# A fused transformer block in fp32: the negative row maxima of the attention are turned behind the second group of value products, in two column groups, and no longer between two score pairs

## The chip, the cores and the metric

The kernel runs on one core of one Trainium2 chip. The metric is the time of one execution in device microseconds (us), as the median of several executions. All arithmetic is in fp32, with fp32r (a rounded fp32) for the large products, which are split into a high and a low part.

## The reference

What is computed is one block with adaptive layer norm: attention with 32 heads of 16 over 2048 rows of 512, then a gated feed-forward part of width 1792.

```python
mod = (_silu(c) @ w_mod).reshape(c.shape[0], 6, 1, -1)
sa, ca, ga, sb, cb, gb = (mod[:, 0], mod[:, 1], ...)
h = _layernorm(x) * (1 + ca) + sa
x = x + ga * attention(h, A_wqkv, A_wo)      # softmax over 2048 keys, 32 heads of 16
h = _layernorm(x) * (1 + cb) + sb
x = x + gb * ((_silu(h @ B_w_gate) * (h @ B_w_up)) @ B_w_down)
```

The softmax is the ordinary one: the maximum of each score row is taken off before the exponential.

## The kernel before, in words

**Tiling.** The attention runs over 32 units. A unit is a group of four heads against 512 queries; it has 16 steps, one for each 128 keys. A step makes four score products (one for each head, L568: keys on the output's partitions, 512 queries along its columns), four exponentials of them on ScalarE (L570) and the value products (L583) that multiply the exponentials with the values. Values and a column of ones are 17 columns of each head, so that a value product has 32 output partitions: the four heads of a group stand beside each other in four column groups of TensorE, each with all 128 rows. A score product has a contraction of 50 rows only and uses half of TensorE's rows.

**The maxima.** The row maxima have to be known ahead of the exponentials. So the kernel computes the scores a second time, 21 steps ahead (`LEAD`), with queries on the partitions: a product on the other half of the rows (L521, 48 rows) into a PSUM bank, and a reduction of that bank on VectorE (L523). There are four banks for these products (numbers 0 to 3, `four`), and three (numbers 4 to 6, `bank`) for the scores whose exponentials ScalarE takes. A *pair* is one score product and one product for a maximum (`pair_of`); the two stand in different halves of TensorE's rows and run side by side.

**Windows.** `plain` runs steps in which there is no other product to fill TensorE with. It goes by windows: three pairs (`WIN`), then one or two half steps of value products (`pvs`; a half step is four matmuls), then what is due at the end of a step (`end_steps`). Over four windows the half steps are 2, 2, 1, 1, so four windows are three steps, and the four windows are called W1 (followed by eight value products), W2 (followed by eight), W3 (followed by four) and W4 (followed by four) below. `filled` runs steps between whose pairs products of the output projection and the feed-forward part are taken.

**Turning the maxima.** When the last maximum of a unit is known, every query has its maxima in one column of `m` (128 partitions by 16). The scores take them off inside the product: two more rows of the contraction (rows 48 and 49 of `qop`) hold minus the maximum as a rounded part `nm` and the rest, and the key operand has ones there. So 16 columns of 128 have to become rows. Where a step has filler, VectorE does that (`max_turned`). Where it has none, `max_rows` does: VectorE takes the maximum over four blocks (L528), ScalarE makes the rounded negative (L540), and three TensorE matmuls with 16 stationary columns (L533 to L535) write the rounded part and the rest into two column ranges of one bank of the three for the scores; ScalarE copies the bank (L537) and SyncE's queue sends two small DMAs into `qop` (L539). The work is put into the list `side`, of which one entry is taken after each pair: the three matmuls come behind the fifth entry's pair, thus two pairs into the second window after the maximum, with the third pair behind them.

**Order.** The instructions of each engine stand in the order in which this code issues them; nothing moves them later. An engine runs its queue in that order, and waits where an operand or a bank isn't ready.

Of the kernel before, what the change touches and what calls it, by code (L numbers as in the profile page):

```python
# [9 lines left out]
F32 = mybir.dt.float32  # L10
F32R = mybir.dt.float32r
# [8 lines left out]
P = 128  # L20
# [18 lines left out]
KR = 48  # L39
# [20 lines left out]
def take(it, k):  # L60
    run(islice(it, k))
# [40 lines left out]
def block_kernel(ctx, tc, x, wqkv, wo, w_gate, w_up, w_down, c, w_mod, out):  # L102
    nc = tc.nc
# [18 lines left out]
    four, bank, single = Turn(0, 1, 2, 3), Turn(4, 5, 6), Turn(7)  # L122

    ident = const.tile([P, P], F32, name="ident")
    minus = const.tile([P, P], F32, name="minus")
# [228 lines left out]
    bank = Turn(4, 5, 6, 7)  # L354
# [101 lines left out]
    for ci in range(NC - 1):  # L456
# [6 lines left out]
        if ci == 1:  # L463
            bank = Turn(4, 5, 6)
# [25 lines left out]
    pb = ctx.enter_context(tc.tile_pool(name="pb", bufs=2, reuse_waits="tile"))  # L490
    kop[1] = pb.tile([P, 2, S], F32R, name="kop1", bufs=1)
    pf = None
    qop, mx, pts, pv, o_, due, res = {}, {}, {}, {}, {}, {}, {}
    posts = []
    n = 16 * NU
    last = NC - 1

# [27 lines left out]
    def max_rows(u):  # L525

        m = pb.tile([P, 16], F32, name="m", tag="m")
        nc.vector.tensor_reduce(m, mx.pop(u).rearrange("p b s t f -> p (b s t) f"), op=ALU.max, axis=AX.X)  # L528
        nm = pb.tile([P, 16], F32R, name="nm", tag="nm")

        def rows():
            pr = bank("pr")[0:16, 0:2 * P]
            nc.tensor.matmul(pr[:, 0:P], nm.bitcast(F32), ident, start=True, stop=True)  # L533
            nc.tensor.matmul(pr[:, P:2 * P], m, minus, start=True, stop=False)  # L534
            nc.tensor.matmul(pr[:, P:2 * P], nm.bitcast(F32), minus, start=False, stop=True)  # L535
            mr = pb.tile([16, 2, P], F32R, name="mr", tag="mr", bufs=1)
            nc.scalar.copy(mr, pr.rearrange("p (r q) -> p r q", r=2))  # L537
            for r in range(2):
                nc.sync.dma_start(qop[u][KR + r:KR + r + 65:64].bitcast(F32), mr[:, r, :].bitcast(F32))  # L539
        side.extend([lambda: None, lambda: None, lambda: nc.scalar.mul(nm, m, -1.0), lambda: None, rows])  # L540

    def max_turned(u, scale=nc.scalar.mul):

# [28 lines left out]
    def pv_step(i, half):  # L572

        u, kt = divmod(i, 16)
        g = u % NG
        cols = slice(half * HQ, (half + 1) * HQ)
        if kt == 0 and half == 0:
            pv[u] = single("pv")
            o_[u] = pf.tile([P, CW], F32, name="o", tag="o", bufs=2)
        p_ = pts.pop(i) if half else pts[i]  # L580
        for h in range(4):
            e0 = (kt * H + 4 * g + h) * (DH + 1)
            nc.tensor.matmul(pv[u][32 * h:32 * h + 32, cols], v_flat[:, e0:e0 + 32], p_[h][:, cols],  # L583
                             start=(kt == 0 and half == 0), stop=(kt == 15),
                             skip_group_check=half == 1)
        if kt == 15 and half:
            nc.scalar.copy(o_[u], pv[u])
# [285 lines left out]
    side = []  # L873
# [20 lines left out]
    def hook():  # L894
        while posts:
            posts.pop(0)()
# [7 lines left out]
    four, bank = Turn(0, 1, 2, 3, 6, 7), Turn(4, 5)  # L904
# [4 lines left out]
    def close_unit(u, i):  # L909

        if u == NU - 1:
            res[u] = out_a(u, nc.scalar)
            return
        res[u] = out_a(u, nc.sync)
        if u + 3 < NU:
            load_k(u + 3)
            load_q(u + 3)
        i0 = i if u % NG == NG - 1 else i + 3
        at(i0 + 3, lambda: res.__setitem__(u, out_b(u, nc.sync, *res[u])))
        at(i0 + 4, lambda: res.__setitem__(u, out_r(u, nc.sync, *res[u])))  # L920
        at(i0 + 5, lambda: out_c(u, nc.gpsimd, nc.gpsimd, *res.pop(u)))
        if u % NG == NG - 1:
            if u // NG:
                at(i + 4, lambda: begin(u // NG))
                at(i + 5, lambda: chunks[u // NG].load_wo())
            at(i + 7, lambda: chunks[u // NG].load_o(nc.gpsimd))
            at(i + 9, lambda: chunks[u // NG].split_o())
# [7 lines left out]
    def after(i):  # L935
        nonlocal pf
        for f in due.pop(i, []):
            f()
        j = i + LEAD
        if j % 16 == 15 and j < n:  # L940
            if i < -1:
                max_turned(j // 16, nc.vector.tensor_scalar_mul)
            else:
                (max_turned if beside else max_rows)(j // 16)
        if i == -2:
            run(late)
            sm.finish()
            es_a0.close()
            pf = ctx.enter_context(tc.tile_pool(name="pf", bufs=1, side="right", reuse_waits="tile"))
            kop[2] = pf.tile([P, 2, S], F32R, name="kop2")  # L950
            ones_rows(2)
            load_k(2)
            load_q(2)
        if 0 <= i < UG and i % 16 in ((3, 5, 8) if i < UG - 16 else (1, 3, 5)):
            next(weights2, None)
# [5 lines left out]
    def pair_of():  # L961
        nonlocal done
        i = done // 4 - 1
        most = 4 * n - 4 * (LEAD - 1)
        h = (ORDER if done < most else (0, 1, 2, 3))[done % 4]
        work = [lambda: score(i + 1, h)]
        if done < most:
            work.insert(1 - h % 2, lambda: max_one(done + 4 * (LEAD - 1)))
        for f in work:
            f()  # L970
        done += 1
        if side:
            side.pop(0)()

    for i in range(-LEAD, -1):
# [7 lines left out]
        if i == -2:  # L983
            four, work = three, bank
            for k in range(4):
                bank = Turn(7, 3, 6)
                for _ in range(WIN):
                    pair_of()
                bank = work
# [6 lines left out]
    def pvs(most, by_halves):  # L996

        nonlocal owed
        if by_halves:
            most, owed = most + owed, 0  # L1000
        while most and halves and 4 * halves[0][0] + 8 <= done:
            i, half = halves.pop(0)
            pv_step(i, half)
            most -= 1
            if i % 16 == 15 and half:
                close_unit(i // 16, done // 4 - 1)
                if by_halves:
                    break
        if by_halves and most and halves and 4 * halves[0][0] + 8 <= done:
            owed = most  # L1010

    def end_steps():
        nonlocal ended
        while ended < done // 4:
            after(ended - 1)
            ended += 1

    def plain(steps, tails=()):

        nonlocal four, bank, beside  # L1020
        beside = False
        assert steps % WIN == 0 and done % 4 == 0
        four, bank = Turn(0, 1, 2, 3), Turn(4, 5, 6)
        for w in range(4 * steps // WIN):
            for _ in range(WIN):
                pair_of()
            if w >= 4 * steps // WIN - len(tails):
                tails[w - 4 * steps // WIN](four())
            pvs((HALVES[(w - 2) % 4] if done > 8 else 0) + (w == 4 * steps // WIN - 1), True)
            end_steps()  # L1030

    def filled(places, work):

        nonlocal four, bank, beside
        beside = True
        four, bank = three, Turn(4, 5)
        if done >= 4 * n - 4 * (LEAD - 1):
            places, bank = ALONE.get(places, places), Turn(4, 5, 0, 1, 2)
        for r in range(len(places)):
            pair_of()  # L1040
            take(work, places[r])
            if r % 4 == 3:
                end_steps()
        hook()
        pvs(6, False)

    def two_of(u):
        return [kop[u % 3][:, e, :].rearrange("p (k c) -> p k c", k=NK) for e in range(2)]
# [11 lines left out]
    for ci in range(last):  # L1060
        plain(STARTS[ci] - done // 4)
        ch = chunks[ci]
        for t0 in (0, 2):
            work = out_pair(ch, t0, outs, True)
            filled(TWO, work)
            filled(TWO, work)
        side.append(lambda: scaled(ch))
        plain(NORM)
        plain(WIN, [lambda tp, k=k: ch.turned(tp, k) for k in range(NK)])
        if ci == last - 1:  # L1070
            plain(REST)
        for _ in range(len(ch.jobs) - (KEEP if ci == last - 1 else 0)):
            job, args = ch.jobs.pop(0)
            if args == (NF // FG - 1, 0):
                plain(WIN)
            work = job(ch, *args, outs, True)
            for places in (TWO, TWO) if job is gate_up else (DOWN,):
                filled(places, work)
# [80 lines left out]
```

## Time and profile before

| what | value |
|---|---|
| median of 3 runs | 1838.07 us (1837.73 to 1839.37) |
| the profiled execution | 1838.88 us, its span on the core 1837.1 us |
| granted TensorE clock | 1.0 of full speed in the profiled span |
| turns by `max_rows` (L533 to L535) | 16 of 32 units, between 203.4 and 1457.5 us |
| mean of one reduction for a maximum (L523) | 681 ns, 2048 of them |

How to read it: the span is the time from the first to the last instruction on the core; what lies around it is start and end of the execution. In the profile an engine's busy time is the union of its instructions. A fp32 matmul of the turn or of the values stands as two records (two passes), a score product as one. The timeline merges consecutive instructions of one form: "x42" is a run of 42, its time runs from the first one's start to the last one's end, and a bracket shows the idle time ahead of it and what ended it. Names such as PE, PEld, DVE, ACT, POOL and SP are TensorE's matmuls, its weight loads, VectorE, ScalarE, GpSimd and SyncE.

### The profile page before, as it was taken

The page shows a single profiled execution, that of the slowest core. Times are in us where ns is not written, and L with a number is a line of the kernel's source. Part 1 is how long each engine was busy: PE and PEld are TensorE (multiplying, and loading weights), DVE is VectorE, ACT ScalarE, POOL GpSimd, SP SyncE. Part 2 cuts the span into 40 slices and gives each one's busy share as a digit, 9 for nine tenths or more (in the row PEclk, how much of TensorE's full clock was granted, in tenths as well). Part 3 has the DMA queues.
Part 4 walks back from the last instruction along what each step waited for, and adds up shares of the span by engine and source line. Part 5 has one row for each costly group of instructions (what it writes and reads, how often), then busy time and mean ns, then how long its engine had stood idle before and what let it go on. Part 6 is the DMA issues. An engine that isn't in the chain of part 4 may idle for free.

```text
span 1837.1 us, 41048 instructions
## 1 busy us (share of the span) xinstructions
PE 1825.5 (99%) x16904; PEld 1198.2 (65%) x16904; DVE 1532.5 (83%) x2578; ACT 1243.7 (68%) x2386; POOL 460.4 (25%) x541
## 2 busy tenths in 40 slices
PE   9999999999999999999999999999999999999999
PEld 7876444444455777776565777776564577777887
DVE  5578999999999888889999888889999988831544
ACT  4223888888877777777878777777878877774211
POOL 3612544565223111111123111111123011130200
PEclk9999999999999999999999999999999999999999
DMA  8884876657845444453544554444643545333642
GB/s 305 286 225 149 183 185 199 168 189 178 209 79 125 102 120 141 118 147 70 149 103 105 134 132 116 123 117 90 158 81 57 111 93 149 138 122 121 271 169 110
DMA packets 80488, 267.63 MB, mean 146 GB/s; under 512 B 19604, under 2 KB 24212, under 8 KB 59620
## 3 DMA queue, kind: packets, MB, share of 16 engines
q1 hardware_dynamic: 61324, 179.71, 33.8%
q0 software_dynamic: 18288, 84.49, 19.3%
q8 instruction: 133, 2.18, 0.5%
q10 hardware_dynamic: 688, 0.80, 0.2%
q14 instruction: 55, 0.45, 0.1%
HBM read 201.85 MB, written 62.13 MB: 144 GB/s over the span
## 4 chain that ended last, share of the span: by engine, by line
PE 96%; DVE 2%; ACT 1%; DMA 1%; SPq 0%; issue 0%; DVEq 0%
PE bank L583 27%; PE bank L781 19%; PE bank L568 18%; PE bank L521 14%; PE bank L791 8%; PE bank L211 7%; DVE mx L523 1%; PE bank L824 1%; DMA wm_ab<-in_w_mod 1%; PE bank L765 0%; DVE stt L807 0%; PE bank L533 0%; PE bank L163 0%; PE bank L534 0%; PE bank L535 0%
## 5 line engine op out<-in xcount | busy, mean ns | idle before, releaser
L523 DVE TENSOR_REDUCE mx<-bank 128x1 f32<-128x512 f32 x2048 | 1276.0, 681 | 108.5 <-PE bank L521 66.2
L568 PE MATMUL bank<-qop,kop 50*128 50x512 f32 x2048 | 730.2, 425 | 1.0 <-ACT pt__16517 L570 0.2
L521 PE MATMUL bank<-kop,qop 48*128 48x512 f32 x2048 | 726.6, 425 | 2.9 <-DVE mx L523 2.6
L568 PEld LDWEIGHTS bank<-qop,kop 50*128 50x128 f32 x2048 | 342.6, 184 | 169.9 <-issue 55.6
L521 PEld LDWEIGHTS bank<-kop,qop 48*128 48x128 f32 x2048 | 343.5, 184 | 113.9 <-DVE mx L523 67.7
L781 PE MATMUL bank<-act,wgu 64*128 64x512 f32 x1872 | 300.9, 392 | 0.0
L781 PEld LDWEIGHTS bank<-act,wgu 64*128 64x128 f32 x1872 | 196.1, 187 | 24.7 <-issue 0.2
L610 POOL TENSOR_TENSOR on<-o,rb 128x512 f32<-128x512 f32 x31 | 39.8, 1284 | 498.1 <-DMA rb<-d_dr 363.6
L781 PE MATMUL bank<-wd,mid 64*128 64x512 f32 x912 | 134.0, 397 | 0.0
L843 POOL CAST mid<-m 128x512 fp32r<-128x512 f32 x40 | 24.3, 608 | 379.3 <-DVE m L841 176.5
L781 PEld LDWEIGHTS bank<-wd,mid 64*128 64x128 f32 x912 | 88.0, 185 | 15.9 <-ACT first L878 3.2
L211 PE MATMUL bank<-hT,wqs 128*128 128x512 f32 x384 | 94.3, 397 | 0.4 <-DVE wqs L351 0.4
L839 DVE SCALAR_TENSOR_TENSOR q<-th,bank 128x512 f32<-128x512 f32 x56 | 38.2, 682 | 54.4 <-ACT th L835 54.4
L211 PEld LDWEIGHTS bank<-hT,wqs 128*128 128x128 f32 x384 | 70.7, 188 | 18.8 <-issue 2.9
L835 ACT ACTIVATE th<-bank 128x512 f32<-128x512 f32 x56 | 33.3, 594 | 58.1 <-PE bank L791 58.1
L855 DVE TENSOR_TENSOR x<-bank,x 128x512 f32<-128x512 f32 x84 | 53.9, 685 | 18.3 <-PE bank L781 16.8
L841 DVE TENSOR_TENSOR m<-bank,q 128x512 f32<-128x512 f32 x56 | 38.7, 691 | 21.7 <-PE bank L791 19.7
L844 POOL TENSOR_TENSOR mid<-m,mid 128x512 fp32r<-128x512 f32 x40 | 51.5, 1287 | 3.3
L791 PE MATMUL bank<-wd,mid 128*128 128x512 f32 x216 | 51.4, 393 | 0.0
L211 PE MATMUL bank<-wqs,hT 128*128 128x512 f32 x192 | 48.0, 398 | 0.0
L781 PE MATMUL bank<-wgu,act 64*128 64x512 f32 x288 | 47.8, 394 | 0.1
L791 PEld LDWEIGHTS bank<-wd,mid 128*128 128x128 f32 x216 | 40.3, 188 | 9.1 <-POOL mid L844 0.3
(6298 smaller groups left out, 5133.0 us busy)
## 6 DMA issues: line engine op xcount, KB each, us to landing
wgu<-gu_dr SPq DMA_DIRECT2D x48, 1024.0 KB
wd<-wd_dr SPq DMA_DIRECT2D x28, 1024.0 KB
kop<-kd SPq DMA_DIRECT2D x33, 768.0 KB
kop<-kd POOLq DMA_DIRECT2D x29, 768.0 KB, 8.8
gu_dr<-wgu POOLq DMA_DIRECT2D x14, 1024.0 KB, 13.5
kd<-prt SPq DMA_DIRECT2D x16, 512.0 KB
qd<-prt SPq DMA_DIRECT2D x16, 512.0 KB
kop<-gu_dr SPq DMA_DIRECT2D x8, 1024.0 KB
```

The lines of the kernel that those rows point to most:

```text
L211: nc.tensor.matmul(pt, lhs(a, k), rhs(b, k), start=(n == 0), stop=(n == 3 * nk - 1))
L521: nc.tensor.matmul(pm, qop[u][rows, s, qt * P:(qt + 1) * P], kop[u % 3][rows, s, kc * CW:(kc + 1) * CW], start=True, stop=True)
L523: nc.vector.tensor_reduce(mx[u][:, b, s, qt, kc:kc + 1], pm, op=ALU.max, axis=AX.X)
L568: nc.tensor.matmul(sp, kop[u % 3][rows, h // 2, kt * P:(kt + 1) * P], qop[u][rows, h // 2, :], start=True, stop=True)
L583: nc.tensor.matmul(pv[u][32 * h:32 * h + 32, cols], v_flat[:, e0:e0 + 32], p_[h][:, cols], start=(kt == 0 and half == 0), stop=(kt == 15), ...
L610: mul.tensor_mul(on, o, rb)
L781: nc.tensor.matmul(outs[e], lhs(e, a, k)[rows], rhs(b, k)[rows], start=(ph == 0 and j == 0), stop=(j == z and (ph == 1 or trade is not None)),
L791: nc.tensor.matmul(outs[e], lhs(e, a, k), rhs(b, k), start=(j == 0), stop=(j == z))
L839: nc.vector.scalar_tensor_tensor(q, th, 1.0, outs[0], op0=ALU.add, op1=ALU.mult)
L841: nc.vector.tensor_mul(m32, outs[1], q)
L844: (nc.gpsimd if slow else nc.vector).tensor_sub(mid[:, 1, :], m32, mid[:, 0, :].bitcast(F32))
L855: nc.vector.tensor_add(ch.x2[:, t, :], outs[e], ch.x2[:, t, :])
```

## The change

`rows`, the part of `max_rows` with the three matmuls, is no longer an entry of `side`. It is put into a new list `behind` with a count of 2; `plain` and `filled` call `turns_behind` behind each group of value products, which counts down and runs it at 0. So the matmuls now stand behind the second group of value products after the maximum. The two results go to two column groups instead of two column ranges: the rest to output partitions 32 to 47, the rounded part to 0 to 15, and the order of the three matmuls is rest, rounded, rest. The copy on ScalarE is 48 partitions by 128 columns instead of 16 by 256. Lines behind L540 have numbers one higher in the changed kernel (L568 is L569, L583 is L584).

```diff
-    posts = []
+    posts, behind = [], []
...
         def rows():
-            pr = bank("pr")[0:16, 0:2 * P]
-            nc.tensor.matmul(pr[:, 0:P], nm.bitcast(F32), ident, start=True, stop=True)
-            nc.tensor.matmul(pr[:, P:2 * P], m, minus, start=True, stop=False)
-            nc.tensor.matmul(pr[:, P:2 * P], nm.bitcast(F32), minus, start=False, stop=True)
-            mr = pb.tile([16, 2, P], F32R, name="mr", tag="mr", bufs=1)
-            nc.scalar.copy(mr, pr.rearrange("p (r q) -> p r q", r=2))
+            pr = bank("pr")[:, 0:P]
+            nc.tensor.matmul(pr[32:48], m, minus, start=True, stop=False)
+            nc.tensor.matmul(pr[0:16], nm.bitcast(F32), ident, start=True, stop=True)
+            nc.tensor.matmul(pr[32:48], nm.bitcast(F32), minus, start=False, stop=True)
+            mr = pb.tile([48, P], F32R, name="mr", tag="mr", bufs=1)
+            nc.scalar.copy(mr, pr[0:48])
             for r in range(2):
-                nc.sync.dma_start(qop[u][KR + r:KR + r + 65:64].bitcast(F32), mr[:, r, :].bitcast(F32))
-        side.extend([lambda: None, lambda: None, lambda: nc.scalar.mul(nm, m, -1.0), lambda: None, rows])
+                nc.sync.dma_start(qop[u][KR + r:KR + r + 65:64].bitcast(F32), mr[32 * r:32 * r + 16].bitcast(F32))
+        side.extend([lambda: None, lambda: None, lambda: nc.scalar.mul(nm, m, -1.0)])
+        behind.append([2, rows])
...
+    def turns_behind():
+        for b in list(behind):
+            b[0] -= 1
+            if not b[0]:
+                b[1]()
+                behind.remove(b)
...
             pvs((HALVES[(w - 2) % 4] if done > 8 else 0) + (w == 4 * steps // WIN - 1), True)
+            turns_behind()
             end_steps()
...
         hook()
         pvs(6, False)
+        turns_behind()
```

The order on TensorE at the first turn (before: 203.4 us of the span). Here the second window is W1, eight value products follow it, and `bank_67` to `bank_69` are the three banks of the scores. Before:

```order
L521 MATMUL bank_66<-kop_1509,qop 128x512
L568 MATMUL bank_67<-qop,kop_88 128x512
L568 MATMUL bank_68<-qop,kop_88 128x512
L521 MATMUL bank_63<-kop_1509,qop 128x512
L533 MATMUL bank_69<-ident,nm 16x128
L534 MATMUL bank_69<-minus,m 16x128
L535 MATMUL bank_69<-minus,nm 16x128
L568 MATMUL bank_67<-qop,kop_88 128x512
L521 MATMUL bank_64<-kop_1509,qop 128x512
L583 MATMUL bank_70<-pt__1774,v_flat 32x256
```

The three matmuls stand between the second and the third pair of the window here. The same place with the change, from the end of W1's eight value products to the third pair of W2:

```order
L584 MATMUL bank_70<-pt__1787,v_flat 32x256
L584 MATMUL bank_70<-pt__1799,v_flat 32x256
L533 MATMUL bank_67<-minus,m 16x128
L534 MATMUL bank_67<-ident,nm 16x128
L535 MATMUL bank_67<-minus,nm 16x128
L521 MATMUL bank_65<-kop_1509,qop 128x512
L569 MATMUL bank_68<-qop,kop_88 128x512
L521 MATMUL bank_66<-kop_1509,qop 128x512
L569 MATMUL bank_69<-qop,kop_88 128x512
L569 MATMUL bank_67<-qop,kop_88 128x512
```

The three matmuls have moved by one pair and eight value products; the third score of the next window now takes the bank that the turn has used.

The third turn (before: 282.1 us), where the second window is W4 with four value products behind it. With the change:

```order
L521 MATMUL bank_64<-kop_971,qop 128x512
L521 MATMUL bank_65<-kop_971,qop 128x512
L569 MATMUL bank_68<-qop,kop_1509 128x512
L584 MATMUL bank_70<-pt__2772,v_flat 32x256
L584 MATMUL bank_70<-pt__2792,v_flat 32x256
L584 MATMUL bank_70<-pt__2777,v_flat 32x256
L584 MATMUL bank_70<-pt__2797,v_flat 32x256
L533 MATMUL bank_69<-minus,m 16x128
L534 MATMUL bank_69<-ident,nm 16x128
L535 MATMUL bank_69<-minus,nm 16x128
L521 MATMUL bank_66<-kop_971,qop 128x512
```

Before, the three stood ahead of the pair with `bank_65`; now that pair and the four value products are ahead of them, and W1 follows.

On ScalarE one exponential moves ahead of the copy, here at the first turn with the change:

```order
L571 ACTIVATE pt__1832<-bank_67 128x512
L571 ACTIVATE pt__1835<-bank_68 128x512
L571 ACTIVATE pt__1840<-bank_69 128x512
L537 CAST mr<-bank_67 48x128
L571 ACTIVATE pt__1862<-bank_68 128x512
```

Before, the copy came ahead of the third exponential. The orders of VectorE, GpSimd and SyncE's queue are the same as before.

## The prediction

> **What bounds the kernel now.** I read the head of the page first, then the busy time by stretches, with the stretch of windows without filler from 195 to 530 us beside one with filler (605 to 860 us), and then the timelines of VectorE and TensorE around the turns.
>
> ```profile
> span 1837.1 us, 41048 instructions
> PE 1825.5 (99%) x16904; PEld 1198.2 (65%) x16904; DVE 1532.5 (83%) x2578; ACT 1243.7 (68%) x2386; POOL 460.4 (25%) x541
> ...
> core 0: us, PE busy (x) PEld busy (x) DVE busy (x) ACT busy (x) POOL busy (x), PEclk, DMA share, GB/s
> 195.00:530.00 335.00, 334.84 (x3364) 161.70 (x3368) 332.86 (x568) 292.37 (x577) 168.73 (x172) 1.00 0.68 180
> 605.00:860.00 255.00, 255.00 (x2710) 187.77 (x2701) 225.82 (x370) 181.14 (x347) 38.01 (x45) 1.00 0.50 124
> ...
> L533 PE MATMUL bank<-ident,nm x32: 272/278/283, 203.4 to 1457.5; 128*16 128x128 f32 x32
> ```
>
> The 99% of PE says little: with filler it is 100% too, and VectorE (DVE) has 29 us of 255 to spare there. Without filler VectorE is idle for 2.1 us of 335. So in the stretches where the turns stand it is VectorE's chain of reductions that sets the time, and TensorE only costs what it makes VectorE wait. The 32 records of L533 are 16 turns of two passes; by their starts all 16 lie in such stretches, between 203 and 1457 us. [...]
>
> What VectorE waits, turn by turn:
>
> ```profile
> L523 DVE TENSOR_REDUCE mx<-bank 128x1 f32<-128x512 f32 x2048 | 1276.0, 681 | 108.5 <-PE bank L521 66.2 <-PE bank L568 34.1
> ...
> 202.26 3.67 DVE L523 TENSOR_REDUCE mx<-bank 128x1 f32<-128x512 f32 x6
> ...
> 206.14 25.35 DVE L523 TENSOR_REDUCE mx<-bank 128x1 f32<-128x512 f32 x42 [0.21 <-PE bank L568]
> 246.31 25.32 DVE L523 TENSOR_REDUCE mx<-bank 128x1 f32<-128x512 f32 x42 [0.24 <-PE bank L521]
> ...
> 280.75 26.15 DVE L523 TENSOR_REDUCE mx<-bank 128x1 f32<-128x512 f32 x43
> ...
> 565.74 9.41 DVE L523 TENSOR_REDUCE mx<-bank 128x1 f32<-128x512 f32 x15
> ```
>
> Six reductions in a row take 3.67 us and the last one 0.68, so one follows the other after (3.67 - 0.68) / 5 = 0.598 us, 0.08 us before its forerunner's record ends. A bracket of 0.21 us therefore is a loss of 0.29, and a run of n that lasts longer than 0.598 (n - 1) + 0.68 has lost the rest inside. By where the turn falls in the four windows there are four kinds:
>
> - **A**, turn in W1 (203.4, 320.4, 437.3, 1457.4 us; 4 of 16): 0.29 + (25.35 - 25.20) = 0.44 us.
> - **B**, in W3 (244.0, 360.9, 477.9; 3): 0.24 + 0.08 + (25.32 - 25.20) = 0.44.
> - **C**, in W4 (282.1, 399.1, 516.0, 921.9, 1327.9, 1419.2; 6): 26.15 - (42 x 0.598 + 0.68) = 0.35.
> - **D**, in W3 of the short stretches that begin with a layer norm (566.6, 972.5, 1378.5; 3): 9.41 - (14 x 0.598 + 0.68) = 0.36.
>
> Together 1.76 + 1.32 + 2.10 + 1.08 = 6.26 us. That is all there is to win on VectorE.
>
> **The change part by part.** What a turn costs TensorE, in a place of kind C:
>
> ```profile
> 281.69 0.39 PE L568 MATMUL bank<-qop,kop 50*128 50x512 f32 x1
> 282.14 0.39 PE L533 MATMUL bank<-ident,nm 128*16 128x128 f32 x2
> 282.37 0.38 PE L534 MATMUL bank<-minus,m 128*16 128x128 f32 x2
> 282.59 0.38 PE L535 MATMUL bank<-minus,nm 128*16 128x128 f32 x2
> 282.90 0.50 PE L521 MATMUL bank<-kop,qop 48*128 48x512 f32 x1
> ...
> 212.99 0.61 PE L521 MATMUL bank<-kop,qop 48*128 48x512 f32 x2
> 213.22 0.40 PE L568 MATMUL bank<-qop,kop 50*128 50x512 f32 x1
> ```
>
> From pair to pair it is 282.90 - 281.69 = 1.21 us with a turn and 0.23 without one (212.99 to 213.22): about 0.95 us are **removed**. What is **added** behind value products:
>
> ```profile
> 212.10 0.38 PE L583 MATMUL bank<-pt__1870,v_flat 128*32 128x256 f32 x1
> 212.11 0.38 PE L583 MATMUL bank<-pt__1890,v_flat 128*32 128x256 f32 x1
> ...
> 212.32 0.38 PE L583 MATMUL bank<-pt__1870,v_flat 128*32 128x256 f32 x1
> ...
> 212.65 0.50 PE L521 MATMUL bank<-kop,qop 48*128 48x512 f32 x1
> ```
>
> Products of different column groups start 0.01 us apart, and the next four 0.22 us behind; then a pair comes after 0.33. A turn there starts 0.22 us behind the last four, its first two matmuls stand in different column groups and share 0.22 us (one matmul's step, 282.37 to 282.59), and the pair comes 0.31 us after the third (282.59 to 282.90). So 0.22 + 0.22 + 0.31 - 0.33 gives a delay of **0.42 us**. Its bounds: not under 0.42, since the first and the third matmul share a column group and its bank; 0.64 if the two don't overlap.
>
> What this delay does depends on how long a bank has lain ready before its reduction begins, its lead:
>
> ```profile
> 205.61 0.49 PE L521 MATMUL bank<-kop,qop 48*128 48x512 f32 x1
> ...
> 214.55 0.73 PE L521 MATMUL bank<-kop,qop 48*128 48x512 f32 x2
> ...
> 215.26 6.66 DVE L523 TENSOR_REDUCE mx<-bank 128x1 f32<-128x512 f32 x11
> ...
> 216.35 0.46 PE L568 MATMUL bank<-qop,kop 50*128 50x512 f32 x1
> 216.81 0.49 PE L568 MATMUL bank<-qop,kop 50*128 50x512 f32 x1
> 217.47 0.38 PE L583 MATMUL bank<-pt__1926,v_flat 128*32 128x256 f32 x1
> 217.80 0.50 PE L521 MATMUL bank<-kop,qop 48*128 48x512 f32 x1
> 218.28 0.18 PEld L568 LDWEIGHTS bank<-qop,kop 50*128 50x128 f32 x1 [0.18 <-ACT pt__2007 L570]
> ...
> L528 DVE TENSOR_REDUCE m<-mx x16: 204/206/220, 202.1 to 1456.1; 128x16 f32<-128x64 f32 x16
> ```
>
> The least lead is 206.14 - (205.61 + 0.49) = 0.04 us. In windows without a turn the first bank of W2 is ready at 212.65 + 0.50 = 213.15; it is the 13th of the run from 206.14, so its reduction begins at 206.14 + 12 x 0.598 + 0.15 = 213.47: lead 0.32. The first bank of W3 is ready at about 214.55 + 0.50 = 215.05 and reduced at 215.26: lead 0.21. That is the tightest place, 0.17 us above the least, since two groups of eight products lie before it. In W4 TensorE is ahead and waits for banks: the third pair comes 216.81 - 216.35 = 0.46 us behind the second instead of 0.23. In W1 its third score waits 0.18 us for an exponential, which costs about 0.08 of the window. So:
>
> - **A now** stands between W1's eight products and W2. Nothing absorbs the delay up to W3: loss 0.42 - 0.17 = 0.25 us (0.14 at W2, 0.11 at W3). Gain 0.44 - 0.25 = 0.19.
> - **C now** stands between W4 and W1. W4's wait is behind it; W1's wait for the exponential absorbs about 0.08. Loss 0.42 - 0.08 - 0.17 = 0.17; gain 0.18.
> - **B and D now** stand between W3 and W4. There W4's wait of 0.23 absorbs it, and so does the 0.21 us by which the maximum over four blocks (L528) has just put VectorE back and lengthened every lead: 0.44 for 0.42. Loss 0; gain 0.44 and 0.36.
>
> Sum: 4 x 0.19 + 6 x 0.18 + 3 x 0.44 + 3 x 0.36 = 0.76 + 1.08 + 1.32 + 1.08 = **4.2 us**.
>
> The rest is costed at nothing, with its cover:
>
> ```profile
> 217.56 0.67 ACT L570 ACTIVATE pt__2007<-bank 128x512 f32<-128x512 f32 x1
> ...
> 283.00 0.36 ACT L537 CAST mr<-bank 16x256 fp32r<-16x256 f32 x1
> ...
> L539 SPq DMA_DIRECT2D qop<-mr x32: 525/538/565, 204.7 to 1459.2; - x32
> ```
>
> *The copy* began 0.41 us behind the third matmul (282.59 to 283.00) and took 0.36 us; with half the columns it lies between this and 0.23 us (the 16 columns of `nm`), and I take 0.25. The third score of the next window now waits for it. Laid onto the rows at 217: turn at 217.69, third matmul 217.91, copy from 218.32 (the exponential before it ended at 218.23) to 218.57, or 218.68 at most; the third score is due at 217.91 + 0.31 + 0.57 = 218.79, and a score started 0.05 us after the exponential it waited for. That leaves 0.06 to 0.17 us of cover. Each 0.1 us beyond it costs about 0.1 per turn of kinds A and C. *The DMAs* are the same two in the same place of SyncE's queue. At most a pair and eight products later, some 1.3 us, they land for scores that come five steps later, 20 reductions or 12 us; each issue takes 0.54 us. *The negative* (L540) ends before and TensorE no longer waits for it.
>
> The profiled execution took 1838.88 us, 0.81 over the median of 1838.07: 1838.88 - 4.2 = 1834.7 there, and **1833.9 us** against the median.
>
> **The rivals.**
>
> 1. *TensorE is the bound after all.* Then each turn is worth 0.95 - 0.42 = 0.53 us, 8.5 in all: 1829.6. For it: PE at 99%. Against it: VectorE's 2.1 idle us in 335. Chance 0.04.
> 2. *Everything VectorE loses comes back*, if TensorE's waits absorb more than I count in A and C: 6.26 us, 1831.8. The waits for banks in W1 and W4 speak for it, the two groups of eight products behind them against it. Chance 0.13.
> 3. *The two column groups don't overlap*: delay 0.64. A loses 0.47, C 0.39, B and D about 0.03 (0.64 - 0.44 - 0.17): 1.88 + 2.34 + 0.18 = 4.4, gain 1.9, 1836.2. Against it: the value products' starts 0.01 us apart. [...] Chance 0.13.
> 4. *Slower: the third score waits for ScalarE's copy*, because exponentials stand before it. With one more (0.49 us, less the cover of 0.06) each turn delays TensorE by 0.43 us more: A loses 0.68, C 0.60, B and D, with 0.25 of it absorbed, about 0.2: 2.7 + 3.6 + 1.2 = 7.5 instead of 6.26, so 1839.3; with two more, about 8 us on top, 1847. It outweighs the gain from about 0.35 us of delay on. For it: ScalarE runs back to back in W4 (217.56 to 218.23). Against it: that exponential ends before the copy could begin. Chance 0.08.
> 5. *It is hidden*: what VectorE gains is waited for where stretches with filler begin: 1838. Against it: they begin with TensorE at work, not with a DMA. Chance 0.07. That the turns don't move at all is excluded by the order, where 16 of 16 have moved.
>
> **How the numbers follow.** The forecast has 0.55. Its own range is 1832.8 to 1835.2: leads may be off by 0.1 us in the ten turns of A and C, and the cover may be short. About 0.2%, 3.7 us, is what a measurement of this kernel tells from no change, that is 1834.4; two thirds of the forecast's chance (0.37) lie below it. Faster is 0.37 + 0.04 + 0.13 = 0.54, the same 0.18 + 0.13 + 0.07 = 0.38, slower 0.08. The range for 8 in 10 goes from the second rival, 1831.6, to just above the third, 1836.8.
>
> **What would show it.** In the profile of the changed kernel: two of the three matmuls start within 0.02 us of each other or of their passes, and the pair comes 0.75 us after the last four products; brackets of 0.2 us on VectorE are gone behind B and D, while short losses at W2 and W3 stay behind A and C; VectorE's idle time from 195 to 530 us falls from 2.1 us to under 1. The step on the cover is wrong if the third score behind a turn waits for `mr`; the whole is wrong if VectorE's losses go and the span doesn't follow.

## The result, and the profile after

The changed kernel takes **1835.25 us** (median of 15 executions, 1832.86 to 1838.74), the kernel before 1838.93 us (15 executions, 1837.72 to 1840.53): a ratio of **0.9981, 95% interval 0.9974 to 0.9988**, thus 3.7 us or 0.19% less. A later series of the same two kernels gave 1836.39 against 1838.61, 0.9985 (0.9976 to 0.9994). The forecast was 1833.9, its range 1831.6 to 1836.8.

VectorE got back more than was forecast, and a wait that had been priced at nothing took part of it away. The head of the page of the changed kernel, and its busy time by stretches (the whole stretch of windows without filler, then the same from 217.3 us on):

```profile
span 1833.9 us, 41048 instructions
PE 1821.6 (99%) x16904; PEld 1199.0 (65%) x16904; DVE 1530.4 (83%) x2578; ACT 1241.4 (68%) x2386; POOL 460.8 (25%) x541
...
core 0: us, PE busy (x) PEld busy (x) DVE busy (x) ACT busy (x) POOL busy (x), PEclk, DMA share, GB/s
195.00:530.00 335.00, 333.30 (x3360) 161.47 (x3360) 331.60 (x568) 290.76 (x576) 168.69 (x172) 0.99 0.67 180
217.30:530.00 312.70, 312.59 (x3166) 151.46 (x3164) 312.30 (x535) 274.29 (x544) 151.42 (x158) 1.00 0.68 180
```

Over the whole stretch VectorE is idle for 3.4 us, more than the 2.1 before. From 217.3 us on it is idle for 0.4 us of 312.7. So everything that went wrong there lies ahead of 217.3 us, at the first turn.

The best measure of one turn is the time from one maximum over the four blocks (L528) to the next, since the same reductions lie between. The starts of the first five, before:

```profile
202.12 0.22 DVE L528 TENSOR_REDUCE m<-mx 128x16 f32<-128x64 f32 x1
242.27 0.21 DVE L528 TENSOR_REDUCE m<-mx 128x16 f32<-128x64 f32 x1
280.62 0.21 DVE L528 TENSOR_REDUCE m<-mx 128x16 f32<-128x64 f32 x1
319.06 0.22 DVE L528 TENSOR_REDUCE m<-mx 128x16 f32<-128x64 f32 x1
359.22 0.20 DVE L528 TENSOR_REDUCE m<-mx 128x16 f32<-128x64 f32 x1
```

And with the change:

```profile
201.14 0.22 DVE L528 TENSOR_REDUCE m<-mx 128x16 f32<-128x64 f32 x1
244.26 0.22 DVE L528 TENSOR_REDUCE m<-mx 128x16 f32<-128x64 f32 x1
282.17 0.21 DVE L528 TENSOR_REDUCE m<-mx 128x16 f32<-128x64 f32 x1
320.26 0.22 DVE L528 TENSOR_REDUCE m<-mx 128x16 f32<-128x64 f32 x1
360.24 0.21 DVE L528 TENSOR_REDUCE m<-mx 128x16 f32<-128x64 f32 x1
```

The first interval (kind A) went from 40.15 to 43.12 us. The next is B, 38.35 to 37.91: 0.44 less. Then C, 38.44 to 38.09: 0.35 less. Then an A that nothing disturbs, 40.16 to 39.98: 0.18 less. An undisturbed first turn would have taken 39.98, so its trouble cost 43.12 - 39.98 = 3.1 us. The two profiled executions differ by 3.2 us of span. That is 1.0 us ahead of the first maximum (202.12 to 201.14, where nothing is changed), less 0.5 us lost between there and the maximum of the ninth turn, and 2.7 us from it to the end.

The turn itself, on TensorE of the changed kernel at the third turn (kind C):

```profile
284.30 0.38 PE L584 MATMUL bank<-pt__2772,v_flat 128*32 128x256 f32 x1
...
284.52 0.27 PE L534 MATMUL bank<-ident,nm 128*16 128x128 f32 x1
284.52 0.27 PE L533 MATMUL bank<-minus,m 128*16 128x128 f32 x1
...
284.74 0.38 PE L535 MATMUL bank<-minus,nm 128*16 128x128 f32 x2
285.05 0.50 PE L521 MATMUL bank<-kop,qop 48*128 48x512 f32 x1
```

The first two matmuls start at the same 284.52, the third 0.22 us later, and the pair comes 285.05 - 284.30 = 0.75 us behind the last four products. This is the delay that was forecast, to the digit.

And the first turn, two windows later. TensorE's timeline, where the bracket is the idle time ahead of a row and what ended it:

```profile
209.51 0.49 PE L569 MATMUL bank<-qop,kop 50*128 50x512 f32 x1
211.59 0.47 PE L569 MATMUL bank<-qop,kop 50*128 50x512 f32 x1 [1.59 <-DMA qop<-mr]
...
213.27 0.79 PE L521 MATMUL bank<-kop,qop 48*128 48x512 f32 x1
```

VectorE's timeline of the same place:

```profile
212.13 1.29 DVE L523 TENSOR_REDUCE mx<-bank 128x1 f32<-128x512 f32 x2 [0.93 <-PE bank L521]
214.09 1.89 DVE L523 TENSOR_REDUCE mx<-bank 128x1 f32<-128x512 f32 x3 [0.67 <-PE bank L569]
217.26 1.89 DVE L523 TENSOR_REDUCE mx<-bank 128x1 f32<-128x512 f32 x3 [1.28 <-PE bank L521]
```

The first score that needs the turned rows waits 1.59 us for the DMAs that bring them. From 213.2 to 216.6 us the granted clock of TensorE stands at 0.5 (half clock from here on), and the product at 213.27 takes 0.79 us instead of 0.49. VectorE loses 1.01, 0.75 and 1.36 us (each bracket and the 0.08 of its overlap), which makes up the 3.1 us. The first is the wait; the other two come while the clock is down.

### The profile page after: what moved, and what is told of

The parts are those of the page before. It is cut to its first block, busy times and chain, and to the rows that moved or that the text cites. A ratio compares the mean times of both kernels' runs of the same rounds, so it can differ in the third digit from the quotient of the medians.

```text
span 1833.9 us, 41048 instructions
## 1 busy us (share of the span) xinstructions
PE 1821.6 (99%) x16904; PEld 1199.0 (65%) x16904; DVE 1530.4 (83%) x2578; ACT 1241.4 (68%) x2386; POOL 460.8 (25%) x541
## 4 chain that ended last, share of the span: by engine, by line
PE 82%; DVE 16%; DMA 1%; ACT 0%; issue 0%; SPq 0%; DVEq 0%
PE bank L584 21%; PE bank L782 19%; DVE mx L523 15%; PE bank L569 14%; PE bank L521 11%; PE bank L792 8%; PE bank L211 7%; PE bank L825 1%; PE bank L766 0%; DMA wm_ab<-in_w_mod 0%; DVE stt L808 0%; DMA qop<-mr 0%; PE bank L163 0%; DVE v_flat L856 0%; PE bank L535 0%
## 5 line engine op out<-in xcount | busy, mean ns | idle before, releaser
L569 PE MATMUL bank<-qop,kop 50*128 50x512 f32 x2048 | 728.8, 426 | 2.5 <-DMA qop<-mr 1.6
L569 PEld LDWEIGHTS bank<-qop,kop 50*128 50x128 f32 x2048 | 343.5, 184 | 169.8 <-issue 53.6
```

The costliest lines, as they stand in the source:

```text
L569: nc.tensor.matmul(sp, kop[u % 3][rows, h // 2, kt * P:(kt + 1) * P], qop[u][rows, h // 2, :], start=True, stop=True)
```

## The experiments

The question was what the two parts of the change do alone, and what the wait costs. The theory: the rows' DMAs, issued later, now land after they are needed, and at the first turn a large transfer of GpSimd's queue makes that a wait. The rival: the place behind the products is itself worse for turns of kind A, and the DMA only shows it. The runs stand in three series, each with the kernel before beside them: 1838.78 us (28 executions) for `columns_alone`, `place_alone`, `first_old` and `mixed`; 1839.32 (9) for `late_one`, `after_w135`, `one_row` and `one_row_mixed`; 1838.61 (21) for `before_w135`, `after_again` and `one_row_w135`.

**The parts alone.** `columns_alone` keeps the old place among the pairs and takes only the two column groups:

```diff
-        side.extend([lambda: None, lambda: None, lambda: nc.scalar.mul(nm, m, -1.0)])
-        behind.append([2, rows])
+        side.extend([lambda: None, lambda: None, lambda: nc.scalar.mul(nm, m, -1.0), lambda: None, rows])
```

> The turns stay between the score pairs as before, but go to two column groups (the first two of the three matmuls share their time). Theory 1 (VectorE's losses set the time, and a turn's delay to TensorE decides them): the turn is 0.22 us shorter, each turn's loss falls by about 0.22 us (A and B 0.44 to 0.22, C and D 0.35 to 0.14), so 3.4 us less than before, ratio 0.9981; the rows land 0.2 us earlier than before, so no turn waits for its DMA. Rival (the place alone makes the gain, the column groups are idle decoration): same as before, ratio 1.000.

`place_alone` moves the turn, with the old three matmuls in one column group (the list `behind` and `turns_behind` are as in the change and left out here):

```diff
-        side.extend([lambda: None, lambda: None, lambda: nc.scalar.mul(nm, m, -1.0), lambda: None, rows])
+        side.extend([lambda: None, lambda: None, lambda: nc.scalar.mul(nm, m, -1.0)])
+        behind.append([2, rows])
```

> The turns stand behind the second group of value products, as in the change, but in one column group and two column ranges as before (three matmuls one after the other). Theory 1: a turn delays TensorE by 0.64 us instead of 0.42; kind A loses about 0.49 us, C under 0.1, B and D nothing, so 2.2 instead of 6.3 us on VectorE, a gain of 4 us; the wait of the first turn for its DMA (1.6 us in the profile of the change) stays, so 2 to 3 us less than before in the median, ratio 0.9984 to 0.9989. Rival (the column groups make the gain): no gain, ratio 1.000.

`columns_alone` took 1834.64 us, ratio 0.998 (0.9972 to 0.9989), as expected. `place_alone` took 1838.80, ratio 1.0000 (0.9991 to 1.0009), where a gain of 0.11 to 0.16% had been expected. Its turn on TensorE shows the serial matmuls, 0.22 us each, and VectorE a bracket at W2 of the next A turn:

```profile
282.15 0.38 PE L533 MATMUL bank<-ident,nm 128*16 128x128 f32 x2
282.37 0.38 PE L534 MATMUL bank<-minus,m 128*16 128x128 f32 x2
282.59 0.38 PE L535 MATMUL bank<-minus,nm 128*16 128x128 f32 x2
282.90 0.50 PE L521 MATMUL bank<-kop,qop 48*128 48x512 f32 x1
...
322.18 25.40 DVE L523 TENSOR_REDUCE mx<-bank 128x1 f32<-128x512 f32 x42 [0.26 <-PE bank L569]
```

In `columns_alone` the first two matmuls overlap between pairs as well, the second pass of each 0.12 us behind its first:

```profile
280.66 0.28 PE L533 MATMUL bank<-minus,m 128*16 128x128 f32 x1
280.76 0.28 PE L534 MATMUL bank<-ident,nm 128*16 128x128 f32 x1
280.78 0.27 PE L533 MATMUL bank<-minus,m 128*16 128x128 f32 x1
280.88 0.27 PE L534 MATMUL bank<-ident,nm 128*16 128x128 f32 x1
280.89 0.38 PE L535 MATMUL bank<-minus,nm 128*16 128x128 f32 x2
281.20 0.50 PE L521 MATMUL bank<-kop,qop 48*128 48x512 f32 x1
```

The intervals between the starts of L528, in us, of the first four turns in one profiled execution each (marked where TensorE waited for the rows):

```
kernel          A (first)   B       C       A
before          40.15       38.35   38.44   40.16
the change      43.12*      37.91   38.09   39.98
columns_alone   39.91       38.15   38.14   39.93
place_alone     40.46*      38.05   38.29   40.25
first_old       40.04       37.90   38.07   39.96
mixed           40.09       37.89   38.07   39.92
one_row         39.75       37.89   38.08   39.75
```

So the two column groups help A, B and C (0.20 to 0.30 us; D has no interval in the table). The place helps B and C, and with serial matmuls it harms A (40.25 against 40.16). Both together bring B and C to within 0.02 us of the lowest in the table. In the medians the column groups alone are worth as much as the whole change, 4.1 us against 3.7: what the move of the place adds at B and C is lost again as long as the first turn waits. `place_alone` had two waits for the rows, 0.15 us at the first turn and 0.85 at the fifth (the timeline names an exponential for the second, but that had ended 0.43 us before; the landing of the rows was signalled at 366.61 us and the score started at 366.70), and two stretches at half clock, 561.7 to 568.5 us and one at 1374.1. By its undisturbed intervals A, B and C gain 3 x 0.30 + 6 x 0.15 - 4 x 0.09 = 1.4 us, and its time shows none of it; that these disturbances took it is likely from the profile but is not shown.

**The first turn put back.** `first_old` leaves the first turn, and `mixed` all four A turns, at the old place, with the column groups everywhere:

```diff
-        behind.append([2, rows])
+        if done < 64:
+            side.extend([lambda: None, rows])
+        else:
+            behind.append([2, rows])
```

> As the change, but the first turn alone (unit 1) stands in its old place, behind the second pair of its window, in two column groups. Theory 1 with a late DMA (the first turn's rows leave 1.3 us of TensorE's order later, meet the store of the prepared weights on the DMA engines, land 6.2 us after their issue and make TensorE wait 1.6 us; its clock is then halved for 3.4 us): without that wait the median is 5.0 us under the kernel before, ratio 0.9973, and most executions show a mean clock of 0.999 or more. Rival (the spread of the change's times has nothing to do with the first turn): ratio 0.998 as for the change, with times spread over 5 us as there.

In `mixed` the condition is another one:

```diff
-        behind.append([2, rows])
+        if done % 4:
+            behind.append([2, rows])
+        else:
+            side.extend([lambda: None, rows])
```

> As the change, but all four turns of kind A (units 1, 4, 7 and 28) stand in their old place, in two column groups; B, C and D behind the value products. Theory 1: kind A loses about 0.22 us there instead of 0.28 behind the eight products, and the first turn's DMA is in time; 5.2 to 5.6 us less than before, ratio 0.9970 to 0.9972, the fastest of these. Rival (place doesn't matter for A beyond the first turn): the same as first_old within 0.3 us.

`first_old`: 1833.07 us, 0.997 (0.9958 to 0.9981), with no wait for the rows in its profile. `mixed`: 1835.08, 0.9973 (0.9964 to 0.9981). It had been expected to be the faster of the two, and the intervals don't tell them apart. In the table an A turn at the old place takes 39.92 against 39.96 to 39.98 behind the products: 0.05 us for each of three turns is under what these times tell apart. So the rival falls: with column groups both places are worth nearly the same to A, and what matters is the first turn.

**The wait, from three sides.** `late_one` makes the rows still later, behind the third group of products:

```diff
-        behind.append([2, rows])
+        behind.append([3, rows])
```

> As the change, but the turns stand behind the third group of value products, one window (about 1.8 us) later. This tells how much cover the rows' DMAs have left. In the change the first score that needs the rows starts 3.8 us (B and D), 4.9 (C) and 5.0 us (A) after the issue, and the rows land after 2.0 us where the DMA engines are free. Theory 1: the first scores then need them after about 2.0 (B and D), 3.0 (C) and 3.2 us (A): B and D wait up to 0.3 us in most turns, and where the weights are stored at the same time TensorE waits a microsecond or more; slower than the change, ratio 0.998 to 1.000. Rival (the DMAs have cover to spare and the one wait of the change was an accident): A loses nothing there and C 0.28, so 0.9975 to 0.998 without any wait for a DMA.

`after_w135` leaves the turns as the change has them and moves GpSimd's preparation of weights, which sends the large transfers, in the early units; `before_w135` is that edit on the kernel before:

```diff
-        if 0 <= i < UG and i % 16 in ((3, 5, 8) if i < UG - 16 else (1, 3, 5)):
+        if 0 <= i < UG and i % 16 in (1, 3, 5):
```

> As the change, but the preparation of the weights on GpSimd is called at steps 1, 3 and 5 of a unit instead of 3, 5 and 8, so its stores of 1 MB leave earlier than the rows of a turn. Theory 1: the rows of the first turn land about 2 us after their issue instead of 6.2, TensorE doesn't wait for them, and the median comes down to that of the executions of the change at full clock, 4.8 to 5.2 us under the kernel before, ratio 0.9973. Rival (the wait has another cause than the stores): the first turn waits as before, ratio 0.998.

> The kernel before, with the preparation of the weights at steps 1, 3 and 5 as in after_w135 and the turns as before. Theory 1: before, no turn waited for its DMA (the rows landed at 5.2 us at the first turn, needed at 6.3), so moving the weights brings nothing by itself: within 0.7 us of the kernel before, ratio 0.9996 to 1.0004. Rival (the earlier weights are a gain of their own, apart from the turns): 1 to 2 us less, ratio 0.9990 to 0.9995.

`late_one`: 1848.01 us, 1.0049 (1.0036 to 1.0062), slower and much more than expected. `after_w135`: 1832.82, 0.9964 (0.995 to 0.9978), no wait for the rows. `before_w135`: 1838.68, 0.9998 (0.9989 to 1.0007): the edit by itself brings nothing, so what `after_w135` has over the change goes with the wait. The intervals of the two ratios touch (0.995 to 0.9978, and 0.9974 to 0.9988 for the change), but the first interval between L528 does not leave it open: 39.97 us in `after_w135`, 43.12 and 42.99 in the two profiles of the change. `after_again` is the changed kernel once more beside `before_w135`:

> The changed kernel once more, for a second profile and more times. Theory 1: the first turn's rows meet the store of the weights again and land between 4 and 7 us after their issue, with TensorE waiting wherever that is over 5.0 us; its executions at full clock lie near 1833.5 us, the others 1 to 5 us above. Rival (the wait was an accident of one execution): rows at 2 us, no wait, and a median near 1833.5.

It took 1836.39 us and shows the wait at the same turn (1.45 us, until 212.18), and two shorter ones of 0.19 and 0.31 us.

The view of waits has one line for the scores that wait for the rows: us in total, times, the longest. First the changed kernel:

```profile
PE bank L569 <- DMA qop<-mr: 1.6, 1, 1.6
```

Then `late_one`:

```profile
PE bank L569 <- DMA qop<-mr: 8.3, 9, 1.9
```

8.3 us of waits, and with them three stretches at half clock, one of double length, against a median that is 8.7 us over the kernel before. `late_one` also tells what half clock adds to a wait. Two of its waits, 0.99 and 1.48 us at turns of kind C, were followed by no half clock: their intervals are 39.17 and 39.65 us, against 38.37 for an undisturbed C there, thus 0.80 and 1.28 us longer. In the change waits of 1.59 and 1.45 us with half clock behind them lengthened the interval by 3.1 and 3.0.

Why the rows are late at the first turn is read from the queues. GpSimd and SyncE's queue in the changed kernel:

```profile
204.69 0.60 POOL L650 DMA_DIRECT2D wo_dr<-wgu  x1 [0.30 <-POOL wgu L647]
205.28 0.76 POOL L642 DMA_DIRECT2D mid<-in_B_w_up  x1
...
204.85 1.10 SPq L539 DMA_DIRECT2D qop<-mr  x2
```

The same in the kernel before:

```profile
204.67 1.11 SPq L539 DMA_DIRECT2D qop<-mr  x2
...
205.33 0.60 POOL L649 DMA_DIRECT2D wo_dr<-wgu  x1 [0.30 <-POOL wgu L646]
```

And in `after_w135`:

```profile
202.06 0.60 POOL L650 DMA_DIRECT2D wo_dr<-wgu  x1 [0.30 <-POOL wgu L647]
...
205.18 1.10 SPq L539 DMA_DIRECT2D qop<-mr  x2
```

In the change the two small DMAs are issued between a store of 1 MB and a load of 0.5 MB of GpSimd's queue (sizes from the view of DMA issues). In `after_w135` the store is 3 us ahead, and GpSimd issues nothing more before 210.66. From the records of single packets, the us from the first issue to the last packet of the rows, and to the first score that wants them. The semaphore that releases the score comes another 0.3 to 0.5 us behind the last packet:

```
first turn       landed in   needed in   TensorE waited
before           5.18        6.32        -
the change       6.20        5.0         1.59
after_again      6.00        5.0         1.45
after_w135       2.09        4.99        -
first_old        1.97        6.23        -
```

So the rows take 2.0 to 2.1 us where they go 0.77 us or more ahead of the store (`first_old`) or 3 us behind it (`after_w135`, where the busy share of the DMA engines is 0.3 or less from 205.6 to 211.8 us), and 5 to 6 us beside it: from 205.85 to 210.4 us that share is 0.97 in the change and 0.86 before. Before, they were late too, but needed 1.3 us later. How late goes with the lead of the rows' issue over the store's: with 1.01 us (`mixed`), 0.89 (`first_old`) and 0.77 (`columns_alone`) the first turn's rows landed in 1.97 to 2.01 us, with 0.66 (before) in 5.18, with 0.12 (`place_alone`) in 4.73, and 0.16 and 0.24 us behind the store (the change, `after_again`) in 6.20 and 6.00. The need is 3.8 us at turns of kinds B and D in the change, 4.9 at C. In `late_one` it is 2.2 at B and D, 3.0 at C and 3.3 at A, and the semaphore of rows that meet no large transfer comes at 2.3: four of its nine waits, 0.2 us each, are those of B and D. Whether the store or the load holds the rows up was not tried apart.

**One row.** The rest of the maximum can go: the rounded maximum taken off in numerator and denominator cancels in the softmax as the full one does. `one_row` turns only the rounded part (one matmul, 16 rows, one DMA, a contraction of 49 rows):

```diff
-            pr = bank("pr")[:, 0:P]
-            nc.tensor.matmul(pr[32:48], m, minus, start=True, stop=False)
...
+            pr = bank("pr")[0:16, 0:P]
+            nc.tensor.matmul(pr, nm.bitcast(F32), ident, start=True, stop=True)
+            mr = pb.tile([16, P], F32R, name="mr", tag="mr", bufs=1)
+            nc.scalar.copy(mr, pr)
+            nc.sync.dma_start(qop[u][KR:KR + 65:64].bitcast(F32), mr.bitcast(F32))
...
-        rows = slice(64 * (h % 2), 64 * (h % 2) + KR + 2)
+        rows = slice(64 * (h % 2), 64 * (h % 2) + KR + 1)
```

> As the change, but a turn is one matmul: the rounded negative maximum alone is taken off the scores (49 rows of contraction instead of 50), which shifts every score of a query by the same number, so the softmax stays what it was; one DMA instead of two. Theory 1: the turn behind the value products delays TensorE by 0.22 us less than in the change (0.2 instead of 0.42), under the cover of VectorE's leads, so kind A loses under 0.1 us instead of 0.28 and the profile shows almost no loss of VectorE behind any turn; at a full clock 5.7 to 6.2 us less than before, ratio 0.9967 to 0.9972, if no turn waits for its DMA. Rival (VectorE's losses are not what the time follows): the same as the change, ratio 0.998.

> One matmul a turn, and the four turns of kind A in their old place, the others behind the value products. Theory 1: no loss on VectorE in any of the 16 turns, 6.2 us less than before, ratio 0.9966; the rows of the first turn land before they are needed in every execution, so the times spread less than those of the change. Rival (the old place costs the same whatever the length of the turn): kind A loses 0.4 us each, ratio 0.9975.

> One matmul a turn behind the value products (as one_row), and the weights prepared at steps 1, 3 and 5. Theory 1: no loss on VectorE and no wait for a DMA, so it stands at one_row or up to 0.5 us under it: ratio 0.9958 to 0.9966. Rival (both remove the same thing): no different from one_row.

`one_row`: 1832.21 us, 0.9962 (0.9949 to 0.9974). `one_row_mixed`, with the A turns at the old place: 1832.49, the same ratio, so for one row too the place of the A turns decides nothing. `one_row_w135` adds the weights' steps of `after_w135`: **1831.34 us, 0.9958 (0.9946 to 0.9971)**, the lowest here, 7.3 us under the kernel before of its series. Its page and its stretch without filler:

```profile
span 1829.8 us, 40858 instructions
...
195.00:530.00 335.00, 334.84 (x3354) 162.84 (x3354) 334.58 (x573) 292.84 (x582) 159.41 (x167) 1.00 0.70 183
```

VectorE is idle for 0.42 us of 335, the rows land within 2.33 us at every turn, and the clock record stays at 1.0 in all five executions. Next to nothing is left to win from the turns there.

## Why the prediction was right, and the step of it that failed

**The bound: right.** VectorE's losses went and the span followed. The first rival (TensorE as the bound) put 8.5 us on the turns at this delay, where VectorE's sum is 5.3 and no kernel with these turns came to more than 6.5 in its median. The fifth (hidden) is refuted by the ratio.

**The delay of 0.42 us: right**, by the starts at 284.52 and the 0.75 us. The third rival (no overlap) is refuted by the same rows, and `place_alone` shows what it would have been: its A turns lose 0.54 to 0.61 us instead of the 0.47 priced, its C turns 0.20 to 0.22 instead of 0.39. The weight loads run beside a matmul in the same rows too: L533's second one stands at 284.53 us (0.10 us long), L534's first pass at 284.52 to 284.79. One figure of the working is off without harm: from pair to pair the turn cost 1.21 - 0.23 = 0.98 us, not about 0.95, which would put the first rival at 9.0 us.

**Kinds B and D: right.** 0.44 us forecast for B and 0.44 measured; D loses nothing any more but for 0.2 us at 566 us, close behind a stretch at half clock.

**Kind A: right.** Gain 0.19 forecast, 0.18 measured; losses of 0.27 to 0.29 remain at W2 and W3, 0.25 forecast.

**Kind C: a term mis-sized.** Forecast was a loss of 0.17 left and a gain of 0.18 per turn. No loss is left and the gain is 0.35. The 0.21 us by which L528 puts VectorE back was credited to B and D only; it lengthens the leads in the windows behind a C turn as well. Behind C turns the records show leads of 0.31 to 0.34 us in W1, 0.20 to 0.24 in W2 and 0.11 to 0.12 in W3, the tightest place, where the forecast left no more than the least lead of 0.04. Over six turns that is 1.0 us, and it brings VectorE's sum from 4.2 to 5.3 us, between the forecast and the second rival's 6.26.

**The copy: right.** It takes 0.26 us where 0.25 was assumed (`mr` in the changed kernel, ns: least, median, most):

```profile
L537 ACT CAST mr<-bank x16: 259/259/263, 204.6 to 1456.8; 48x128 fp32r<-48x128 f32 x16
```

No score waits for it, so the fourth rival did not happen as it was told.

**The DMAs: the step that failed.** They were costed at nothing because they would "land for scores that come five steps later, 20 reductions or 12 us". The call of `max_rows` comes 14 to 16 pairs ahead of the unit's first score, six of them pass before the moved matmuls run, and so 3.8 to 5.0 us are left, not 12. A landing time from the profile of before would have shown the danger: 5.18 us at the first turn, needed at 6.32, beside a delay of the issue of some 1.3 us. The wait then cost 3.1 us in the profiled execution, 1.0 of it at the wait itself and 2.1 with the clock down. `first_old` and `after_w135`, which take the wait away in two unlike ways, stand at 1833.07 and 1832.82 us, 2.2 to 3.6 us under the change's two medians, and 5.7 and 6.5 us under the kernel before of their series. `mixed` has no such wait either and yet 1835.08: six of its eleven executions have a mean clock under 1.0, and the other five a median of 1832.58. So the intervals at the first turn carry this step, and the medians only support it. The wait is also why the sign that the forecast named, VectorE idle for under 1 us from 195 to 530 us, did not come (3.4).

**What is still open.** The median gain, 3.7 us, is what VectorE regains, 5.3, less what waits and half clock take in many executions. That it lies so near the forecast of 4.2 is luck in part: 1.0 us too little for C and a wait that was put at nothing pull opposite ways. Over both series 8 of 26 executions of the change have a mean clock of 1.0 in the record; their median is 1833.6 us, and that of the other 18 is 1836.2. The kernel before has such others too: 28 of 58 are at 1.0, and the others' median is 1.4, 2.4 and 0.4 us higher in the three series. So its own median holds some of this as well. Half clock also comes near layer norms (about 561, 968 and 1374 us), all three times in `before_w135`, where the turns are the old ones; whether the change makes it more frequent there was not settled.

## What to carry to other kernels

Moving work later on a slack engine moves its DMA later too: find the first reader of that DMA, count the time from issue to reader, and set it against the longest landing time in the profile, not the median. A stall is priced with what follows it, since 1.6 us of idle TensorE cost 3.1 here. When the work goes behind other work of its kind, count the leads afresh behind every stop of the engine that waits, since here the 0.21 us by which L528 stops VectorE were slack for TensorE.

## What the runs showed of the hardware

- Matmuls of 16 stationary columns in two column groups, with the same 128 rows, start together (284.52 and 284.52 us in the change); in one group they follow at 0.22 us (282.15, 282.37 and 282.59 in `place_alone`).
- Two DMAs of 8 KB, from the first issue to the last packet at the first turn: 2.0 us (1.97 in `first_old`) and 2.1 (2.09 in `after_w135`) ahead of GpSimd's store or 3 us behind it; 4.7 (`place_alone`) to 6.2 us (the change) beside 1.5 MB, the store and a load of that queue.
- The granted clock stood at 0.5 for 3.41 us at a time in the change (213.19 to 216.60 and 561.35 to 564.76 us), and for 6.8 us in `place_alone` (561.7 to 568.5). A wait of TensorE of 1.59 us stands ahead of the first of these, one of 1.45 us ahead of the one in `after_again`. In `late_one` waits of 0.99 and 1.48 us were followed by none, and the 3.41 us ahead of the second in the change hold 0.04 us of idle TensorE. So the length of a wait does not decide it alone, and what does was not shown.
